# A new stored order and engine choice for the 2207 pieces of an attention and gated-MLP kernel

## The chip, the core and the metric

The kernel runs on one core of one Trainium2 chip. The metric is device time in microseconds (us) of one execution, as the median of several runs. The core has a matrix engine (TensorE, PE in the profile, its weight loads shown apart as PEld), a vector engine (VectorE, DVE), an engine for functions such as exp and gelu (ScalarE, ACT), a general engine (GpSimd, POOL) and a queue engine that issues transfers (SyncE, SP). Each engine runs its own instructions in the order in which the program gives them; engines wait for each other with semaphores.

## What is computed

There are 8 batches of 8 heads, 576 positions and 64 columns. Attention is taken twice, once over a band of 7 neighbours and once over means of 4 positions, and the two results are added. The output is the input of a gated MLP (512 to 1024 columns, a 576 x 576 product across positions, 512 to 512) with a residual:

```python
q_d = q.reshape(B, H, Sd, factor, D).mean(axis=3)
out_d = sm_attn(q_d, k_d, v_d)
out_up = np.repeat(out_d, factor, axis=2)
mask = np.abs(pos[:, None] - pos[None, :]) < factor
out_local = np.matmul(attn, v)
return (out_up + out_local).astype(np.float32)
```

```python
h = x @ w_in            # then gelu
u, v = (h[..., :d_ff // 2], h[..., d_ff // 2:])
v_n = (v - mu) / np.sqrt(var + 1e-06) * g_ln
v_s = np.einsum('ts,bsd->btd', w_sg, v_n) + b_sg[None, :, None]
gated = u * v_s
return (x + gated @ w_out).astype(np.float32)
```

## The kernel before

**Pieces and order.** The whole work is cut into 2207 named pieces. `add(name, engines, emit, after, takes, gives)` records one: the engines that may do it, the function that writes its instructions, the pieces it must follow and the buffers it takes and frees. A string, `ORDER`, holds all the names in one sequence; `name/V`, `name/A`, `name/P` or `name/S` chooses DVE, ACT, POOL or SP, and a name alone takes the first engine of its dictionary. `place` reads the string and hands out buffers from three pools (`SIZES`: 8 of PSUM, 10 and 40 of SBUF); a buffer is handed to the next piece that wants one in the order of the string. Then the pieces are written out in that sequence, so the string is the order of work on every engine's queue:

```python
for t, e in order:
    t.emit(e)
```

**Attention** runs over 32 pairs of heads, g = 0 to 31, four per batch. `lq`, `lk`, `lv`, `lw` load; `qs`, `ks` (L394 on DVE, else POOL) and `vs` sum groups of four; `YS` (for the first four pairs `Y` and `S`) are the pooled and the banded scores on PE (L447, L427); `ma`, `mb` add the mask (L435), `mx`, `my` take maxima (L458, L468), `nx`, `ny` scale them (L465, L477 on DVE), `ea`, `eb`, `ec` are the exponentials on ACT (L486, L493), `re`, `rc` the reciprocals, `np`, `nq` the normalizations (L507, L510). `T`, `U`, `t` transpose on PE (L513, L523), `pa`, `pb`, `pc`, `pe` copy the results out of PSUM (L226), `d` and `D` are the two products with the values on PE (L559, L580), `od` (L568), `xa`, `xb` (L587) join them. `xh`, `xl` (L599), `xc` split the result into a high and a low part, since each product of the MLP is made of three reduced-precision matmuls.

**The MLP** of batch b has 5 pieces `v` (L681, five tiles of positions; for batch 0 three of them are cut into `vk` and `v`), each followed by gelu (`vg`), statistics (`vb`, L711), a root (`vp`, L722 on POOL), `vn` (L730) and a split `vh`, `vl` (L750); then 8 pieces each of `u`, `s` and `o` (L759, 128 x 288 outputs, 12 to 14 matmuls). `ua` is the gelu of `u` (L777), `sa` the bias of `s` (L796), `sm` the gate (L803), `gh`, `gl` (L815) the split of the gated value, `oa` the residual (L831), `os` the store. Every `o` needs all four `gl` of its batch.

**Weights** come as 64-bit floats and are turned into a high and a low part by `weight64` for each of 24 blocks: `wb` (L301, L303) on DVE, `wu`, `wq` on ACT, `wf` (L318) on DVE, `wt` (L323) on POOL, `wh` (L226) and `wl` (L329) on either of two engines. Letters y, z and r stand for the two halves of the first weight and for the last one. The 576 x 576 weight has five `whq`, `wlq` (L356). All of it is done during batch 0.

So in the first 100 us or so the weights, the attention of batches 0 and 1 and the MLP of batch 0 are interleaved, and later the attention of one batch with the MLP of the one before.

Of the kernel before, what the change touches and what calls it, by code (L numbers as in the profile page):

```python
# [92 lines left out]
wqy6 wuy6 nq0/P T0 re1/V t0 U0 nx2/V pa0/V rc1 ea2 wur3 wuz2 wur0 wbz4 pb0/V qs3/V wqz4 wfy6 pc0/V ks3/V pe0/V S3
mx3 wbz5 wfz4 eb2 wuz3 nx3/A wur7 ea3 wly4/P wly3/P nq1/P np1/P T1 pa1/V U1 wqz5 wly5/P wty6/P d0 qs4/P lv2 re2/V
why6/V t1 pb1/V rc2 wby1 pc1/V od0 wqy1 lq5 Y3 wfz5 pe1/V ks4/P wfy1 D0 np2/P eb3 xa0 xb0 T2 my3 pa2/A wuz5 wur1
wur2 ny3/A wuz1 nq2/P U2 wtz4/P wty1/P YS4 pb2/V xh0/V pc2/V t2 wuz0 why1/A ma4 mb4 wbz7 pe2/A ec3 wqz7 d1 mx4 nx4/A
b lw4 re3/A wq3 eb4 lq6 wly6/P my4 wbz6 d2 xl0/P wly1/P wtz5/P xc0 rc3 lv3 wr4 lk6 od1 lv4 lw3 qs5/P lk5 D1 wbz0
nq3/P wfz7 ny4/V wqz6 np3/P wfz6 wtz7/P od2 xa1 wqz0 wq0 wfz0 D2 xb1 xa2 xh1/V ec4 ea4 re4/A xb2 xl1/V wtz0/P wtz6/P
t3 rc4 np4/V vk2.0 T3 vk1.0 pa3/A wbz2 wur4 wbz1 ks6/V U3 pb3/A pc3/A whz7/A pe3/A vk1.1 vk2.1 xh2/A T4 pa4/A nq4/P
wqz1 U4 wqz2 pb4/A whz6/A wlz7/P d3 pc4/A od3 xc1 t4 xl2/P pe4/A qs6/V ks5/V wfz2 wfz1 vs4 wlz6/V whq3/A whz5/A  # L100
vk1.2 wlz5/P whq2/A whz4/A D3 xa3 xb3 xh3/A whz0/A YS5 xc2 wtz1/P vk0.0 lq7 lk7 wur5 xl3/P lv5 wq4 wq1 wlz4/P xc3
ma5 mb5 mx5 wtz2/P qs7/P my5 wbz3 ny5/V d4 vk0.1 vk2.2 vk0.2 v0.1 v0.2 od4 nx5/A eb5 wbr1 wqz3 wfz3 v0.0 wtz3/P
wlq2/P ec5 whz1/A wqr1 ks7/V D4 ea5 wbr5 v0.4 whz3/A wqr5 whz2/A xa4 wfr1 wbr3 xb4 wr6 lw6 v0.3 re5/A va0.4/A wqr3
wfr5 rc5 wbr2 vj0.4 wfr3 wtr1/P wlz1/P wlz3/P vg0.0 np5/P u0.4 T5 vg0.2 vg0.1 vg0.4 vg0.3 wqr2 whq4/A wlz0/V vb0.0
vb0.2 wlz2/V nq5/P u0.6 ua0.6 ua0.4 whr1/A pa5/A wur6 whq1/A whq0/A vb0.1 YS6 vp0.0 wlq3/P u0.0 U5 xh4/A ua0.0
wlq4/V u0.1 vn0.0 wlr1/V vp0.1 vh0.0/A vn0.1 ma6 vb0.3 wtr5/P t5 wtr3/P wlq0/P whr3/A vh0.1/A ua0.1 whr5/A pb5/A
pc5/A vp0.2 vb0.4 wlq1/V wlr3/V vn0.2 mb6 vp0.4 u0.3 u0.7 u0.2 lq8 lw5 pe5/A vp0.3 vn0.4 vh0.2/A vl0.0/V vh0.4/A
# [10 lines left out]
v1.2 vg1.1 vb1.1 vp1.1 vn1.1 ks10/V pe8/A re9/A rc9 np9/P nq9/P vg1.2 d8 od8 v1.0 vg1.0 vg1.3 vb1.2 vp1.2 D8 u1.0
lv9 os0.1 vb1.0 T9 xa8 vp1.0 vn1.0 vs9 vb1.4 xb8 vb1.3 vp1.4 ks11/V vn1.2 vn1.4 u1.2 ua1.2 U9 u1.3 YS10 ua1.0 pa9/A
vp1.3 vh1.0/A pb9/A lk12 lw10 vh1.4/V ma10 my10 mb10 vn1.3 vh1.3/V pc9/A xh8/V ua1.3 ny10/V vl1.4/V lq12 mx10 nx10/V  # L120
vl1.3/V u1.4 qs12/V t9 ua1.4 u1.1 pe9/A d9 vh1.1/A vh1.2/A od9 ua1.1 u1.5 vl1.1/P qs11/P D9 u1.7 ec10 xl8/P xc8 xa9
xb9 xh9/V vl1.0/V vl1.2/P ks12/V eb10 ea10 YS11 lw11 lv10 u1.6 s1.4 lk13 lq13 my11 ma11 ny11/A ec11 re10/V rc10
np10/V T10 mb11 mx11 xl9/V nq10/P s1.0 U10 pa10/V qs13/V pb10/V pc10/V sa1.0 ua1.5 nx11/A ua1.6 ua1.7 s1.1 sa1.1
ks13/V t10 xc9 vs10 s1.2 sm1.1/P pe10/V d10 sm1.0/V ea11 eb11 re11/A s1.3 sa1.2 sm1.2/P rc11 gh1.0/A s1.5 sa1.4
np11/V lv11 gl1.0/P nq11/V U11 T11 sa1.3 s1.6 od10 t11 pa11/A sm1.4/P pb11/A pc11/A sm1.3/V sa1.5 sm1.5/V gh1.2/A
gh1.1/V gl1.1/V pe11/V sa1.6 vs11 gl1.2/V s1.7 sa1.7 sm1.6/P D10 d11 xa10 xb10 sm1.7/P od11 YS12 gh1.3/A D11 lq14
lv12 ma12 xa11 xb11 mb12 gl1.3/P my12 xh10/V ny12/V vs12 YS13 ma13 mb13 my13 lk14 o1.7 o1.6 o1.2 xh11/A o1.4 lw13
# [847 lines left out]
```

## Time and profile before

| | us |
|---|---|
| median of 3 runs | 598.51 |
| lowest and highest | 598.5 and 599.11 |
| span of the profiled execution | 597.5 |
| PE, DVE, ACT, POOL busy | 574.8, 433.8, 333.1, 319.4 |

The page's rows in tenths cut the span into 40 slices of 14.9 us each. A row of a waits view names who waited, on which line, for whom; a row of a stretches view gives the length of the stretch, then for PE, PEld, DVE, ACT and POOL the busy time and the number of instructions, then the granted clock of PE, the share of the DMA engines and GB/s. A row of the chain of waits has a start, a length and the engine, tile and line, with a count where several instructions stand together. A group row has the engine, operation, output and input, shapes and count, then busy time and the mean ns of one, then the idle time before them.

### The profile page before, as it was taken

The page shows a single profiled execution, that of the slowest core. Times are in us where ns is not written, and L with a number is a line of the kernel's source. Part 1 is how long each engine was busy: PE and PEld are TensorE (multiplying, and loading weights), DVE is VectorE, ACT ScalarE, POOL GpSimd, SP SyncE. Part 2 cuts the span into 40 slices and gives each one's busy share as a digit, 9 for nine tenths or more (in the row PEclk, how much of TensorE's full clock was granted, in tenths as well). Part 3 has the DMA queues.
Part 4 walks back from the last instruction along what each step waited for, and adds up shares of the span by engine and source line. Part 5 has one row for each costly group of instructions (what it writes and reads, how often), then busy time and mean ns, then how long its engine had stood idle before and what let it go on. Part 6 is the DMA issues. An engine that isn't in the chain of part 4 may idle for free.

```text
span 597.5 us, 16612 instructions
## 1 busy us (share of the span) xinstructions
PE 574.8 (96%) x6544; PEld 524.0 (88%) x6544; DVE 433.8 (73%) x926; ACT 333.1 (56%) x1264; POOL 319.4 (53%) x407
## 2 busy tenths in 40 slices
PE   3889998999999999999999999999999999999997
PEld 2577997988999899988999889998999989998997
DVE  5999999867786787745966587964879659753553
ACT  5999974764937357371475547548484635722210
POOL 4888889534764154742765364625766336431330
PEclk9989998999999999999999999999999999999999
DMA  8996105072031150502213432403404030010002
GB/s 307 359 276 195 58 15 172 22 225 84 22 101 67 40 186 1 174 20 82 73 48 122 142 105 64 123 34 104 149 25 147 2 122 23 22 42 20 21 21 80
DMA packets 28494, 58.18 MB, mean 97 GB/s; under 512 B 3328, under 2 KB 3584, under 8 KB 28416
## 3 DMA queue, kind: packets, MB, share of 16 engines
q1 hardware_dynamic: 27840, 55.88, 29.5%
q8 instruction: 52, 0.85, 0.6%
q10 hardware_dynamic: 576, 1.23, 0.6%
q14 instruction: 26, 0.21, 0.1%
HBM read 47.66 MB, written 9.44 MB: 96 GB/s over the span
## 4 chain that ended last, share of the span: by engine, by line
PE 86%; DVE 6%; ACT 4%; issue 2%; POOL 1%; DMA 1%; DVEq 0%; POOLq 0%; ACTq 0%
PE ps L759 49%; PE ps L681 18%; PE ps L580 4%; PE ps L559 3%; PE ps L523 3%; PE ps L513 3%; PE ps L427 3%; PE ps L447 3%; ACT X L486 3%; DMA R<-in_qT_dram 1%; DVE R L803 1%; ACT R L309 1%; DVE vs L796 1%; POOL R L803 1%; DVE R L750 0%
## 5 line engine op out<-in xcount | busy, mean ns | idle before, releaser
L759 PE MATMUL ps<-wsg_h,R 128*128 128x288 f32 x576 | 122.3, 299 | 0.0
L759 PE MATMUL ps<-R,wout_h 128*128 128x288 f32 x512 | 110.1, 301 | 0.0
L486 ACT ACTIVATE X<-X,nb 128x64 f32<-128x64 f32 x280 | 93.5, 339 | 6.0 <-DVE nb L465 5.7
L759 PEld LDWEIGHTS ps<-wsg_h,R 128*128 128x128 f32 x576 | 93.7, 188 | 0.7 <-ACT R L226 0.2
L759 PE MATMUL ps<-wsg_l,R 128*128 128x288 f32 x320 | 92.6, 295 | 0.0
L759 PEld LDWEIGHTS ps<-R,wout_h 128*128 128x128 f32 x512 | 84.1, 189 | 2.2 <-issue 1.0
L759 PE MATMUL ps<-X,win_h 128*128 128x288 f32 x256 | 78.7, 308 | 0.0
L759 PE MATMUL ps<-R,win_h 128*128 128x288 f32 x256 | 75.7, 296 | 0.0
L759 PE MATMUL ps<-R,wout_l 128*128 128x288 f32 x256 | 75.7, 296 | 0.0
L759 PE MATMUL ps<-X,win_l 128*128 128x288 f32 x256 | 75.6, 295 | 0.0
L722 POOL TENSOR_TENSOR rs<-rs,nhalf 128x1 f32<-128x1 f32 (+1 forms) x40 | 24.9, 628 | 79.2 <-DVE rs L713 79.2
L681 PE MATMUL ps<-win_h,X 128*128 128x512 f32 x160 | 65.6, 410 | 0.0
L681 PE MATMUL ps<-win_l,X 128*128 128x512 f32 x160 | 63.1, 395 | 0.0
L759 PEld LDWEIGHTS ps<-wsg_l,R 128*128 128x128 f32 x320 | 60.3, 188 | 0.0
L803 POOL TENSOR_TENSOR R<-R,vs 128x288 f32<-128x288 f32 x31 | 29.6, 963 | 45.1 <-DVE vs L796 40.4
L486 ACT ACTIVATION_READ_ACCUMULATOR X<-X,nb 128x1 f32 x280 | 53.6, 192 | 0.0
L226 ACT COPY R<-ps 72x288 f32<-72x288 f32 (+3 forms) x82 | 32.2, 419 | 37.4 <-PE ps L513 17.4
L796 DVE SCALAR_TENSOR_TENSOR vs<-ps,small_sb,b_sb 128x288 f32<-128x288 f32 x64 | 32.1, 510 | 28.4 <-PE ps L759 24.9
L681 PE MATMUL ps<-win_h,R 128*128 128x512 f32 x128 | 50.6, 395 | 0.0
L759 PEld LDWEIGHTS ps<-X,win_h 128*128 128x128 f32 x256 | 48.2, 188 | 2.1 <-issue 0.6
L759 PEld LDWEIGHTS ps<-R,win_h 128*128 128x128 f32 x256 | 48.3, 189 | 0.3
L759 PEld LDWEIGHTS ps<-R,wout_l 128*128 128x128 f32 x256 | 48.4, 189 | 0.0
(100 smaller groups left out, 1405.9 us busy)
## 6 DMA issues: line engine op xcount, KB each, us to landing
X<-in_vw_dram SPq DMA_DIRECT2D x31, 320.0 KB
R<-in_v_dram SPq DMA_DIRECT2D x64, 144.0 KB
R<-in_kT_dram SPq DMA_DIRECT2D x31, 293.0 KB
out_dram<-R SPq DMA_DIRECT2D x31, 288.0 KB
R<-in_qT_dram SPq DMA_DIRECT2D x30, 293.0 KB
R<-in_w_in_dram SPq DMA_DIRECT2D x16, 256.0 KB
...
```

What stands on the lines that cost most here:

```text
L226: (nc.scalar.copy if e == "A" else ENG[e].tensor_copy)(**kw)
L427: nc.tensor.matmul(out=sp[i][os, c * KB:(c + 1) * KB], lhsT=q[hs, t * QB:t * QB + KB], rhs=k[hs, t * QB:t * QB + KB], start=not early, sto ...
L447: nc.tensor.matmul(out=st["sdv"][n][os], lhsT=qd2[par][hs, i * 48:i * 48 + HD], rhs=st["kd"][hs], start=True, stop=True)
L486: nc.scalar.activation(out=st["ms"][:, t, :], in_=src, func=AF.Exp, bias=st["nb"][:, t:t + 1], scale=scale, accum_out=sums[par][:, t:t + 1])
L513: nc.tensor.matmul(out=out, lhsT=st["ms"][0:LD, 2 * c:2 * c + 2, :], rhs=turn_l, is_transpose=True, start=True, stop=True)
L523: nc.tensor.matmul(out=out[:, i * QD:(i + 1) * QD], lhsT=st["pd"][0:QD, n, keys], rhs=turn_p[:, i % 2], is_transpose=True, start=True, sto ...
L580: nc.tensor.matmul(out=at["ps", "o", g, i][hs, c * QB:(c + 1) * QB], lhsT=v[ks, c, hs], rhs=pt[ks, c, h ^ int(2 * c + i >= NA)], start=Tru ...
L681: nc.tensor.matmul(out=acc, lhsT=r32(l), rhs=r32(w[:, k, DM:DF]), start=(i == 0 and ks[0] == 0), stop=(i == len(ops) - 1 and ks[-1] == KT ...
L722: nc.gpsimd.tensor_tensor(out=rs[0:n], in0=rs[0:n], in1=nhalf[0:n], op=ALU.pow)
L759: nc.tensor.matmul(out=acc[:, 0:HALF], lhsT=r32(l), rhs=r32(r), start=(first and n == 0), stop=(last and n == len(ops) - 1))
L796: nc.vector.scalar_tensor_tensor(out=vsb[i], in0=at["ps", "m", b, "s", i][:, 0:HALF], scalar=g_sb[:, i // 2:i // 2 + 1], in1=b_sb[:, half( ...
L803: ENG[e].tensor_tensor(out=u[:, half(i)], in0=u[:, half(i)], in1=vsb[i], op=ALU.mult)
```

## The change

The string `ORDER` is replaced by another sequence of the same 2207 names, with other engine suffixes on some of them. All functions that write instructions, all dependencies and the pool sizes are as before. In `weight64`, `wt` loses DVE from its dictionary; every `wt` of the old string had `/P`, so the engine is POOL in both. By piece, the counts of engines that change (before to after): `gh` on ACT 18 to 14; `gl` on POOL 13 to 18; `ks` on POOL 11 to 15 and `qs` 15 to 18; `np` on POOL 16 to 19, `nq` 21 to 18; `nx` on ACT 16 to 18, `ny` 17 to 14; `pa` on ACT 25 to 17, `pb` 18 to 21, `pc` 17 to 20; `re` on ACT 24 to 21; `sm` on POOL 31 to 28; `wh` on DVE 3 to 9 (of the 24 fp64 blocks); `wl` on DVE 7 to 11; `xl` on POOL 17 to 19.

The diff, cut to its start, the place of the first MLP's gate (`sa0.7`, `gl0.3`, `o0.6`), and `weight64`:

```diff
--- before.py
+++ after.py
@@ -85,116 +85,114 @@
 
 
 ORDER = """
-wy2 wby2 wy0 wy7 lq0/A lk0/A wby0 wuy0 wuy2 wqy2 wby7 wfy2 wy4 small wqy0 wy3 wy5 lq1/A lk1/S wy1 lk2 lq2 wfy0 wz7
-lq3 wy6 wz5 lv0/S lk3 wz4 wz2 wz6 ks0/V wr3 qs0/P wqy7 wr0 wr2 Y0 wuy7 S0 lq4 lk4 wz3 wr7 wz1 lw0/S wr1 lv1/S wz0
-lw1/A wfy7 wby4 wty0/P wuy4 why0/A wty2/P why2/A wqy4 wty7/P my0 why7/A ny0/A wuy3 wfy4 wby3 wby5 wly0/P mx0 wty4/P
-wuy5 ec0 wqy3 why4/A wfy3 wqy5 ks1/V wfy5 qs1/P wly7/P wuy1 ks2/P qs2/V nx0/A ea0 eb0 S1 wuz7 mx1 wr5 lw2 wq2 wty5/P
...
-vs5 xl4/P wbr6 ec6 wqr7 whr2/A nx6/A wlr5/V wqr6 s0.1 wfr7 sa0.1 wfr6 s0.2 s0.0 s0.4 wqr4 wfr4 s0.3 wtr7/P wtr4/P
-sm0.1/P eb6 ea6 re6/A wbr0 sa0.0 sm0.0/P wlr2/V wqr0 rc6 sa0.2 wfr0 sa0.3 wtr6/P sm0.2/P gh0.0/A gl0.0/V whr4/A
-sm0.3/V s0.5 sa0.4 sa0.5 sm0.4/V whr6/A whr7/A gh0.1/A s0.6 sm0.5/V sa0.6 nq6/V s0.7 gh0.2/A d5 sm0.6/V sa0.7
-sm0.7/V lv6 lk8 np6/P wtr0/P wlr4/P wlr7/P T6 t6 od5 whr0/A gh0.3/A pa6/A D5 YS7 gl0.1/V xa5 gl0.3/V ma7 xb5 gl0.2/P
-lw7 my7 wlr6/P lk9 xh5/A wlr0/P mb7 mx7 U6 nx7/V pb6/V ny7/A ec7 o0.6 o0.7 pc6/V pe6/V o0.3 oa0.6 ks8/V ea7 eb7 lq9
...
-os6.3 sa7.6 sm7.6/P gh7.3/V gl7.3/V o7.6 o7.2 o7.3 o7.1 o7.0 oa7.2 oa7.3 o7.4 oa7.0 oa7.1 oa7.4 o7.5 oa7.6 oa7.5
-os7.0 o7.7 oa7.7 os7.1 os7.3.0 os7.2 os7.3.1
+wy2 wuy2 wby2 wy4 wuy4 wby4 wqy2 wfy2 wty2 wy0 wuy0 lk0/A wqy4 lq0/A qs0/P wy7 small wy3 wby0 lk1/S ks0/V wqy0 wfy0
...
+wqr3 wfr3 wtr5 wur3 wtr3 vb0.0 vp0.0 whq4/A vk1.2 v0.1 vg0.1 vb0.1 wtr7 vk2.2 v0.2 v0.4 va0.4/A vj0.4 vn0.0 qs6/P
+vg0.2 vb0.2 whr3/A v0.3 wlr3/V vp0.2 vg0.3 vb0.3 T5 U5 whq1/A wlq1/V pa5/A vn0.2 wur0 vp0.1 vn0.1 pb5/A pc5/A whr7/A
+wlq4/V vp0.3 vn0.3 u0.0 ua0.0 u0.1 ua0.1 whr5/A u0.4 ua0.4 YS6 ma6 lk8 vg0.4 vb0.4 vh0.0/A vl0.0/P vh0.3/A vl0.3/V t5
+pe5/A mb6 wbr6 wlq3/V vh0.1/A vp0.4 vn0.4 whr2/A xh4/A wlr5/P wqr6 wfr6 u0.6 ua0.6 u0.5 vl0.1/V vh0.2/A vl0.2/V u0.3
+u0.7 ua0.7 vh0.4/A u0.2 vl0.4/V ua0.2 ua0.3 wbr0 wqr0 wlr2/P wbr4 wqr4 mx6 wfr0 ua0.5 wfr4 wtr6 whr6/A vs5 lq8 wlr6/P
+my6 ny6/V wlr7/V ec6 nx6/A qs8/V ea6 wtr0 s0.0 sa0.0 s0.1 sa0.1 sm0.1/V s0.2 whr0/V wlr0/V sm0.0/V gh0.0/V gl0.0/V
+sa0.2 wtr4 whr4/A sm0.2/V s0.3 sa0.3 sm0.3/V d5 wlr4/V od5 eb6 re6/V rc6 np6/V gh0.1/A gl0.1/V s0.4 lv6 vs6 sa0.4
+sm0.4/V s0.6 sa0.6 s0.5 sa0.5 sm0.5/V nq6/P sm0.6/P s0.7 sa0.7 t6 D5 YS7 gh0.2/A sm0.7/V gh0.3/V xa5 xb5 xh5/A lw7 my7
+lq9 T6 U6 pa6/A pb6/V pc6/A pe6/A gl0.2/P gl0.3/V o0.6 xl5/P lk9 ma7 mb7 mx7 xl4/V xc5 ny7/A ec7 d6 lv7 od6 o0.7 oa0.6
+oa0.7 ks8/P os0.3 nx7/A ea7 eb7 re7/A ks9/V D6 lw8 qs9/V xa6 xb6 xc4 rc7 YS8 lk10 my8 lq10 ma8 mb8 mx8 vs7 o0.3 o0.0
+np7/P T7 ny8/A ec8 nq7/P ks10/V qs10/P pa7/V U7 nx8/A ea8 pb7/A t7 pc7/V pe7/A xh6/V xl6/P oa0.0 eb8 re8/A rc8 np8/P
...
@@ -333,7 +331,7 @@
         add(f"wu{t}", {"A": 0.36}, units, [f"w{t}"])
         add(f"wq{t}", {"A": 0.34}, square, [f"wb{t}"])
         add(f"wf{t}", {"V": 0.43}, flush, [f"wq{t}"], takes=keys[1:2], gives=keys[2:])
-        add(f"wt{t}", {"P": 0.75, "V": 0.7}, total, [f"wf{t}", f"wu{t}"])
+        add(f"wt{t}", {"P": 0.75}, total, [f"wf{t}", f"wu{t}"])
         add(f"wh{t}", {"A": 0.36, "V": 0.26}, high, [f"wt{t}"])
         add(f"wl{t}", {"P": 0.9, "V": 0.36}, low, [f"wh{t}"], gives=keys[:2])
```

More of the change, by code (lines that the diff above doesn't have):

```diff
@@ L93 @@
[L93 to L107, printed above, removed]
@@ L118 @@
[L118 to L127, printed above, removed]
@@ new lines @@
+xc12 u2.0 ea15 s2.1 sa2.1 T14 nq14/P re15/A vs14 lq17 rc15 oa1.1 pa14/A U14 pb14/A pc14/V ua2.0 t14 pe14/V ks17/P
+np15/V os1.0 nq15/V ua2.2 sa2.0 sm2.0/V u2.1 ua2.1 sm2.1/P s2.2 sa2.2 d14 lv15 od14 U15 T15 pa15/V pb15/A D14 xa14
+YS16 my16 ny16/V ec16 ma16 mb16 xb14 pc15/A mx16 lq18 nx16/V vs15 eb16 xh14/V xl14/V ea16 lk18 ks18/P qs18/V t15
+pe15/V s2.3 s2.4 qs17/V re16/V gh2.0/A rc16 u2.3 ua2.3 u2.4 ua2.4 d15 lv16 od15 np16/V nq16/V T16 sa2.3 lw16 sm2.2/P
+sa2.4 pa16/V lw15 sm2.4/V U16 vs16 pb16/A pc16/A t16 pe16/A xc13 D15 YS17 lq19 xa15 xb15 ma17 mb17 mx17 nx17/V qs19/V
@@ new lines @@
+eb18 re18/A rc18 vg3.2 lw19 my19 ny19/V ec19 mx19 nx19/A np18/P nq18/V vs18 vb3.2 ea19 xh17/V vp3.2 vn3.2 vl3.0/P v3.3
+o2.7 vg3.3 vb3.3 vp3.3 o2.3 vn3.4 o2.2 oa2.2 ks21/P vn3.3 oa2.3 eb19 vh3.4/A vl3.4/V os2.1 vh3.2/V vl3.2/V vh3.3/A
+vl3.3/V xl17/V qs20/P xc17 U18 T18 pa18/A pb18/V re19/A pc18/A qs21/V rc19 nq19/V o2.4 oa2.4 o2.5 oa2.5 os2.2 o2.6
+oa2.6 o2.0 np19/V oa2.0 s3.1 s3.0 u3.0 t18 T19 pa19/V oa2.7 pe18/A d18 lv19 os2.3 od18 U19 pb19/V sa3.1 t19 ua3.0
+sa3.0 pc19/A sm3.0/V pe19/A vs19 u3.3 u3.1 s3.3 s3.2 u3.2 ua3.2 s3.5 sa3.2 u3.5 ua3.3 o2.1 u3.4 oa2.1 s3.4 ua3.1
@@ L198 @@
+o7.7 o7.0 o7.4 oa7.4 os6.2 o7.5 oa7.5 os7.2 ok3 o7.2 oa7.2 o6.6 o7.3 oa7.3 os7.1 o7.6 oa7.6 oa6.6 oa7.7 os7.3.1 o6.7
+oa6.7 os6.3 ok1 o7.1 os7.3.0 oa7.0 oa7.1 os7.0
 """
```

158 lines of the change are left out of this document (84 added, 74 removed).

## The prediction

> **What bounds the kernel now.** I read the first part of the page for the whole, the page's slices for places, then the waits of the TensorE (PE), the stretches and the chain of waits.
>
> ```profile
> PE 574.8 (96%) x6544; PEld 524.0 (88%) x6544; DVE 433.8 (73%) x926; ACT 333.1 (56%) x1264; POOL 319.4 (53%) x407
> ...
> PE   3889998999999999999999999999999999999997
> ...
> DVE  5999999867786787745966587964879659753553
> ```
>
> PE is busy 96% of a span of 597.5 us, so most of the time can only fall if PE's own pieces get cheaper. But DVE shows a 9 in slices two to seven (15 to 105 us), and nowhere else in a row: there the two engines are level. The waits say how far PE suffers from it:
>
> ```profile
> PE ps L447 <- POOL R L323: 10.0, 1, 10.0
> PE ps L523 <- DVE R L510: 1.9, 1, 1.9
> PE ps L513 <- ACT X L486: 1.6, 1, 1.6
> ...
> PE ps L447 <- DVE vs L796: 0.5, 1, 0.5
> ```
>
> The first is the start (nothing to multiply until 10.0 us). The second and the last belong to the stretch from 95 to 101 us shown below. The others are small and scattered. So of before there are three regimes: start-up to 45 us, a stretch to about 103 us in which DVE and PE are both full, and 490 us in which PE alone counts. The stretches:
>
> ```profile
> 44.00:65.00 21.00, 21.00 (x248) 16.40 (x247) 19.87 (x45) 19.53 (x72) 18.82 (x25) 1.00 0.56 159
> 65.00:95.00 30.00, 30.00 (x271) 29.63 (x271) 28.79 (x58) 22.55 (x70) 25.60 (x29) 1.00 0.18 54
> 95.00:100.40 5.40, 3.22 (x64) 2.20 (x62) 5.40 (x9) 1.95 (x4) 4.30 (x5) 1.00 0.77 220
> 100.40:103.80 3.40, 3.14 (x54) 2.99 (x55) 3.37 (x7) 1.12 (x2) 3.32 (x5) 0.50 0.64 175
> ...
> 131.00:200.00 69.00, 68.75 (x796) 62.52 (x795) 51.01 (x111) 41.51 (x155) 36.07 (x45) 1.00 0.21 64
> ```
>
> The columns after the length are busy time of PE, its weight loads, DVE, ACT and POOL, then the granted clock. From 44 to 100.4 us DVE is busy 19.87 + 28.79 + 5.40 = 54.06 of 56.4 us, in 45 + 58 + 9 = 112 instructions: 0.483 us each, and only 2.3 us free. From 95.0 PE is idle 2.2 of 5.4 us, and the 3.4 us behind that run at half the clock. From 131 us on DVE is busy 51.01 of 69 us: no bound any more. The chain of waits carries the same through single instructions:
>
> ```profile
> 71.32 0.33 DVE wout_l L329
> ...
> 75.56 0.34 DVE wout_l L329
> ...
> 85.95 1.62 DVE wout_l L329
> ...
> 96.01 0.81 DVE R L803 x2
> ...
> 98.60 1.58 DVE R L803
> 100.18 0.44 DVE vs L796
> 100.62 0.04 issue
> 100.66 0.76 PE ps L447 x8
> ...
> 103.64 2.42 PE ps L759 x17
> ```
>
> Two things are to be seen. At 100.66 us PE's scores of head pair 7 (`YS7`) start when DVE has finished `sa0.7`, the last bias of the first batch's gate; the first output product, `o0.6`, follows at 103.64. And one instruction, L329 on the same shape, takes 0.33 us or 1.62 us, L803 0.41 or 1.58: the long ones fall where POOL is busy.
>
> **The change part by part.** The 6544 matmuls, loads and stores are the same; only the stored order and the engine of some pieces differ. I counted both orders.
>
> *PE's switches.* A dense product (u, s, o, v) is cheaper behind another dense product than behind attention in fp32, and the small attention pieces differ too:
>
> ```profile
> 138.36 0.74 PE ps L580 x40
> 139.10 1.79 PE ps L759 x12
> ...
> 141.31 1.60 PE ps L759 x12
> ...
> 217.04 0.58 PE ps L580 x40
> ...
> 315.51 0.29 PE ps L523 x3
> ...
> 316.54 0.41 PE ps L523 x3
> ```
>
> The u product takes 1.79 us behind an A·V (L580) and 1.60 otherwise: 0.19 apart. L580 takes 0.74 behind a dense piece and 0.58 behind scores: 0.16. A transposition (L523) is 0.29 among dense pieces and 0.41 among attention: 0.12 the other way. The new order gathers attention: dense pieces straight behind fp32 attention fall from 48 to 23 (25 x 0.19 = 4.75 us saved), fp32 pieces straight behind `D` or `YS` rise from 15 to 35 (20 x 0.16 = 3.2 saved), and transpositions followed by attention rise from 29 to 69 (40 x 0.12 = 4.8 lost). Sum 3.2 us saved, nearly all behind 103 us, where PE is the bound, so it counts in full. Bounds: 6 us if the transpositions lose only a quarter of it (the other pairs are unseen in before's trace), 0 if they lose half as much again and a fifth less is saved.
>
> *DVE before the first gate.* Up to `sa0.7` before stores 158 words for DVE, the new order 175. PE's work stored ahead of that place is about the same. By name 37 come in and 20 go out. Net of those that cancel: six fp32 casts of weights (`wh`, L226), four `wl` (L329), one `wlq` (L356), three `pe` and two `pa` copies, two gates `sm` (L803), the half-tile `vl0.4` (L750), one `gl` (L815), one `gh` (L226) come in; one `pc` copy, one `nq` (L510) and two `ny` (L477) go out. Prices, mean over the run:
>
> ```profile
> L815 DVE TENSOR_TENSOR R<-R,R 128x576 fp32r<-128x576 f32 x19 | 17.1, 899 | 1.0 <-ACT R L226 0.7
> ...
> L226 DVE COPY R<-ps 72x288 f32<-72x288 f32 x29 | 12.8, 442 | 0.0
> ...
> L510 DVE TENSOR_TENSOR R<-R,rc 128x432 f32<-128x432 f32 x11 | 9.5, 865 | 0.1
> L226 DVE CAST R<-R 128x576 fp32r<-128x576 f32 x14 | 9.2, 661 | 3.5 <-POOL R L803 3.1
> ...
> L477 DVE TENSOR_SCALAR nbd<-stats 128x3 f32<-128x3 f32 x15 | 7.6, 505 | 0.1
> ...
> L226 DVE COPY R<-ps 128x464 f32<-128x464 f32 x7 | 4.4, 632 | 3.6 <-PE ps L513 3.6
> L750 DVE TENSOR_TENSOR R<-R,R 64x512 fp32r<-64x512 f32 x5 | 4.3, 867 | 0.1
> L226 DVE COPY R<-ps 128x116 f32<-128x116 f32 x14 | 3.8, 270 | 3.7 <-PE ps L523 3.4 <-issue 0.3
> ...
> L356 DVE TENSOR_TENSOR wsg_l<-R,wsg_h 128x576 fp32r<-128x576 f32 x2 | 1.5, 758 | 0.0
> ...
> L226 DVE CAST win_h<-R 128x256 fp32r<-128x256 f32 x3 | 0.8, 279 | 0.0
> ```
>
> With the short prices of L329 (0.34) and L803 (0.41): 6 x 0.279 + 4 x 0.34 + 0.758 + 3 x 0.270 + 2 x 0.632 + 2 x 0.41 + 0.867 + 0.899 + 0.661 - 0.442 - 0.865 - 2 x 0.505 = 6.8 us. With the stretch's mean instead, 17 x 0.483 = 8.2. Both are time on an engine that had 2.3 us free in 56.4. I take the lower price, since the new order moves some of this work off POOL, so that fewer of the long cases should arise, and let half of the free time take a part: 6.8 - 1.2 = 5.6 us later at `sa0.7`. Bounds: 1 us (all free time is used, and the long cases shrink by a third) and 9.6 us (20 words at 0.483: the new order has three more DVE words between `sa0.7` and `gl0.3`, which the first o product, `o0.6`, needs). In before that product starts 3 us behind `sa0.7`, so PE cannot pass this place in the new order before DVE does. What the wait holds up: PE's queue is in order, so `YS7`, `T6`, `U6` and everything after them slide with it. The 1.9 us of `t6` and the 0.5 of `YS7` are inside before's 100.66 and so are not saved beside it.
>
> [...]
>
> *The start.* The loads of the first `k` and `q` are issued by ACT behind its first weight pieces, so PE's 10.0 us wait gets longer, by an estimated 0 to 1.7 us. I cost it at nothing: DVE and ACT have weights to convert meanwhile, and DVE is the later one at 100 us. Without that cover it is 1.7 us.
>
> *Behind 103 us.* Before's waits of PE behind that are the scattered ones (1.6 and smaller). I followed the buffers and results of the new order and found about as many places where a result is short of time by a little; I take them as equal, with 2 us either way, the size of the longest above. ACT alternates between exp and gelu 40 times instead of 28:
>
> ```profile
> L493 ACT ACT_TABLE_LOAD x8 | 10.3, 1283 | 6.6 <-DVE nbd L477 6.5
> L777 ACT ACT_TABLE_LOAD x7 | 9.0, 1283 | 0.1
> ```
>
> 12 x 1.283 = 15.4 us more of ACT, beside an ACT that was busy 41.51 of 69 us (131 to 200): hidden, at nothing; if ACT were the bound it would be up to 15.4. [...]
>
> **Sum.** 597.5 + 5.6 - 3.2 + 0 + 0 = 599.9 for the profiled span. The median of the runs, 598.51, stands 1.0 above that span, so 600.9: slower by 0.4%.
>
> **The rivals.**
> 1. *DVE is no later than before* (the other side, faster). The price of contention falls as POOL's pieces move to DVE, and DVE's order lets PE's needs pass first. For it: POOL was busy 25.60 of 30 us beside the long DVE instructions. Against it: the chain ran through DVE from 70 to 100 us, with 17 words fewer. It decides below 3.2 us of extra DVE time at `sa0.7`: at 0 the span is 597.5 - 3.2 = 594.3, and where DVE is early enough that the idle 2.2 us at 95 us and half of the 3.4 us at half clock go too, 594.3 - 2.2 - 1.7 = 590.4, so 591.4 to 595.3 in the median.
> 2. *It cancels.* DVE loses 2 to 4.4 us: 597.3 to 599.7.
> 3. *Contention at its full price, or new waits.* 9.6 us instead of 5.6 at `gl0.3`, and 2 us of new waits: 600.9 + 4.0 + 2 = 606.9.
>
> **How the numbers follow.** Within 0.2% (about what a measurement of this kernel can tell from no change) is 597.3 to 599.7. My forecast (599.7 to 604) has 0.36, rival 3 (604 to 608) 0.14: slower 0.50. Rival 2 has 0.17. Rival 1 has 0.33: this is a sum of differences of engines that are level, and a switch saving at its bound of 6 us or a third fewer long DVE cases would turn the sign. The range leaves out a tenth at each end: 588.6 (rival 1 with 2.8 us more of switches, its bound) to 606.9. The likeliest case's own range is 599.7 to 604.
>
> **What would show it.** Right: PE in the new profile waits on DVE for several us around `T6`, `YS7` and `o0.6`; `o0.6` starts at 107 us or later, from 103.6; DVE shows 9 through 105 us; the stretch behind it is about 3 us shorter for the same work. Wrong: PE passes `o0.6` before 103 us; or the long L329 and L803 become rare; or PE's waits behind 103 us grow by more than 2 us, above all on ACT behind a table load.

## The result: 3.1% slower, and where the profile puts it

| | before | changed order |
|---|---|---|
| median of the runs, us | 598.81 | 617.40 |
| lowest and highest | 598.50 and 600.39 | 615.44 and 620.06 |
| span of the profiled execution | 597.5 | 613.7 |

The ratio is 1.0312, with a 95% interval from 1.0281 to 1.0342. The forecast was 600.9 and its range ended at 606.9. The sign was right; the size, and most of the reasons, were not, so the right sign was luck.

First the page of the changed kernel: busy time, and the slices (40 of 15.3 us) of PE, DVE, ACT and of PE's granted clock.

```profile
PE 574.8 (94%) x6544; PEld 522.9 (85%) x6544; DVE 426.2 (69%) x935; ACT 342.8 (56%) x1261; POOL 321.9 (52%) x420
...
PE   0779999899899999998999999999999999999997
...
DVE  3699999959655787959826876477865787446342
ACT  2599976587634647858524949246762768213100
...
PEclk9879999999999999999999999999999999999999
```

PE is busy for the same 574.8 us as before (its time at half clock included), so in sum the 16.2 us of span that were lost are waits. The first slice has a 0 where before had a 3. Then PE's waits, the largest first (lines are 2 lower than in before):

```profile
PE ps L445 <- POOL qd L396: 17.9, 2, 16.0
PE ps L578 <- ACT od L566: 3.4, 5, 1.6
PE ps L511 <- DVE R L585: 1.9, 1, 1.9
PE ps L418 <- ACT X L484: 1.5, 1, 1.5
PE ps L757 <- ACT R L491: 1.2, 1, 1.2
PE ps L757 <- DVE X L433: 1.1, 2, 0.9
PE ps L445 <- DVE R L316: 1.0, 1, 1.0
```

PE starts at 16.0 us in place of 10.0, and behind that stands a long tail of waits of one or two us, on ACT, DVE and POOL alike. The stretches of the changed kernel:

```profile
15.10:30.00 14.90, 10.91 (x156) 6.84 (x156) 9.86 (x30) 7.14 (x35) 9.84 (x16) 0.90 1.01 324
30.00:44.00 14.00, 11.40 (x160) 8.08 (x161) 13.65 (x36) 12.84 (x76) 11.59 (x15) 0.74 0.75 245
...
131.00:160.00 29.00, 27.77 (x291) 23.91 (x293) 21.96 (x47) 21.62 (x78) 18.70 (x26) 1.00 0.32 107
160.00:200.00 40.00, 39.10 (x496) 36.51 (x487) 23.18 (x50) 19.04 (x71) 24.30 (x32) 1.00 0.25 74
200.00:300.00 100.00, 96.19 (x1137) 87.11 (x1135) 79.34 (x168) 70.07 (x254) 61.43 (x81) 1.00 0.29 93
300.00:400.00 100.00, 98.84 (x1028) 92.78 (x1029) 59.90 (x130) 51.03 (x172) 44.81 (x58) 1.00 0.26 81
400.00:500.00 100.00, 98.07 (x1235) 88.59 (x1234) 74.50 (x163) 58.20 (x218) 53.03 (x71) 1.00 0.28 89
```

And of before, for the same times behind 200 us:

```profile
200.00:300.00 100.00, 98.31 (x1167) 90.56 (x1167) 71.44 (x150) 48.50 (x176) 50.44 (x63) 1.00 0.29 90
300.00:400.00 100.00, 100.00 (x1154) 93.06 (x1153) 72.98 (x148) 58.58 (x245) 48.34 (x61) 1.00 0.28 87
400.00:500.00 100.00, 100.00 (x1155) 90.13 (x1154) 71.99 (x152) 55.17 (x196) 57.10 (x74) 1.00 0.27 87
```

From 131 to 500 us PE idles 1.23 + 0.90 + 3.81 + 1.16 + 1.93 = 9.0 us in the changed kernel and 0.25 + 1.69 = 1.9 in before. ACT's busy time from 200 to 300 us rises from 48.5 to 70.1.

Single pieces can be followed by name through all traces, since the names fix the order on every queue. Two orders can be compared only at a piece ahead of which PE has done the same set of pieces in both. Starts of such pieces, in us, with two of the experiments beside them:

| piece | PE pieces ahead of it | before | changed | e2_head_before | e5_loads_first_lw1_sp |
|---|---|---|---|---|---|
| `Y0`, first scores | 0 | 10.0 | 16.0 | 10.2 | 10.0 |
| `vk2.1` | 30 | 47.1 | 58.3 | 46.5 | 50.5 |
| `v0.4` | 47 | 60.5 | 71.8 | 60.0 | 64.0 |
| `o0.6`, first output product | 75 | 103.3 | 114.1 | 102.4 | 106.9 |
| `d11` | 133 | 176.4 | 188.7 | 178.3 | 181.9 |
| `YS24` | 292 | 386.3 | 402.3 | 391.0 | 394.9 |
| from `o0.6` to the end | | 494.1 | 499.6 | 500.4 | 499.9 |

Of 16.2 us, 11.3 are lost before `vk2.1`, in the first 50 us. From there to `o0.6` nothing is lost (0.5 is won back). The other 5.4 are lost behind `o0.6`, where I had forecast a gain of 3.2, and nearly all of it between `o0.6` and `YS24`. From `vk2.1` to `o0.6` lies most of the stretch in which DVE was to be the bound. It takes 56.3 us in before, 55.8 in the changed kernel and 56.4 in e5_loads_first_lw1_sp; the rows are in this order:

```profile
47.05:103.32 56.27, 53.83 (x614) 48.32 (x612) 53.93 (x107) 42.31 (x134) 49.72 (x58) 0.97 0.35 103
```

```profile
58.33:114.09 55.76, 53.01 (x613) 47.75 (x612) 53.51 (x117) 38.97 (x125) 40.67 (x49) 1.00 0.23 67
```

```profile
50.50:106.88 56.38, 53.39 (x613) 47.72 (x612) 54.55 (x117) 38.81 (x125) 40.65 (x49) 1.00 0.25 73
```

DVE has ten more instructions here and is busy about as long as in before, since some of them became shorter. The gate `sm` and the split `wl` on DVE, in the same stretch, before and then changed:

```profile
L803 DVE TENSOR_TENSOR R<-R,vs 128x288 f32<-128x288 f32 x5 | 5.4, 1086 | 0.0
...
L329 DVE TENSOR_TENSOR wout_l<-R,wout_h 128x256 fp32r<-128x256 f32 x4 | 3.3, 814 | 0.0
```

```profile
L801 DVE TENSOR_TENSOR R<-R,vs 128x288 f32<-128x288 f32 x7 | 3.6, 515 | 0.2
...
L327 DVE TENSOR_TENSOR wout_l<-R,wout_h 128x256 fp32r<-128x256 f32 x4 | 1.9, 470 | 0.0
```

POOL is busy 40.7 us of the stretch in place of 49.7.

### The profile page after: what moved, and what is told of

Same layout as the page of the kernel before. It is cut to its first block, busy times and chain, and to the rows that moved or that the text cites. A ratio compares the mean times of both kernels' runs of the same rounds, so it can differ in the third digit from the quotient of the medians.

```text
span 613.7 us, 16663 instructions
## 1 busy us (share of the span) xinstructions
PE 574.8 (94%) x6544; PEld 522.9 (85%) x6544; DVE 426.2 (69%) x935; ACT 342.8 (56%) x1261; POOL 321.9 (52%) x420
## 3 DMA queue, kind: packets, MB, share of 16 engines
q10 hardware_dynamic: 576, 1.23, 0.5%
## 5 line engine op out<-in xcount | busy, mean ns | idle before, releaser
L757 PE MATMUL ps<-X,win_h 128*128 128x288 f32 x256 | 76.4, 298 | 0.0
L775 ACT ACTIVATE R<-ps 128x288 f32<-128x288 f32 x64 | 24.3, 411 | 60.6 <-PE ps L757 56.5
L801 POOL TENSOR_TENSOR R<-R,vs 128x288 f32<-128x288 f32 x28 | 23.1, 825 | 62.0 <-DVE vs L794 33.6
L224 ACT CAST R<-R 128x512 fp32r<-128x512 f32 (+2 forms) x36 | 22.9, 639 | 49.6 <-DVE R L728 16.9
L679 PE MATMUL ps<-win_h,R 128*128 128x512 f32 x128 | 50.5, 395 | 0.0
```

The lines of the kernel that those rows point to most:

```text
L224: (nc.scalar.copy if e == "A" else ENG[e].tensor_copy)(**kw)
L679: nc.tensor.matmul(out=acc, lhsT=r32(l), rhs=r32(w[:, k, DM:DF]), start=(i == 0 and ks[0] == 0), stop=(i == len(ops) - 1 and ks[-1] == KT ...
L757: nc.tensor.matmul(out=acc[:, 0:HALF], lhsT=r32(l), rhs=r32(r), start=(first and n == 0), stop=(last and n == len(ops) - 1))
L775: nc.scalar.activation(out=us[i // 2][:, half(i)], in_=at["ps", "m", b, "u", i][:, 0:HALF], func=AF.Gelu_apprx_tanh)
L801: ENG[e].tensor_tensor(out=u[:, half(i)], in0=u[:, half(i)], in1=vsb[i], op=ALU.mult)
```

## The experiments

All times are medians; the kernel before was measured again beside each group of experiments.

| run | us | before beside it | ratio, 95% interval |
|---|---|---|---|
| e1_loads_first | 616.48 | 599.05 | 1.0298 (1.0237 to 1.0359) |
| e2_head_before | 606.91 | 599.05 | 1.0130 (1.0101 to 1.0159) |
| e3_tail_before | 610.89 | 599.05 | 1.0194 (1.0159 to 1.0229) |
| e4_four_hoists | 618.63 | 599.05 | 1.0318 (1.0269 to 1.0367) |
| e5_loads_first_lw1_sp | 612.42 | 599.74 | 1.0199 (1.0167 to 1.0230) |
| e6_lw1_sp | 618.21 | 599.74 | 1.0305 (1.0268 to 1.0342) |
| e7_before_loads_late | 602.74 | 599.74 | 1.0049 (1.0029 to 1.0069) |
| e8_before_gate | 600.76 | 599.74 | 1.0019 (1.0002 to 1.0036) |
| e9_tail_old_engines | 651.45 | 599.54 | 1.0863 (1.0822 to 1.0903) |
| e10_old_order_new_engines | 658.06 | 599.54 | 1.0978 (1.0938 to 1.1019) |
| e11_before_u16_later | 598.12 | 599.54 | 0.9966 (0.9948 to 0.9983) |
| e12_consumers_later | 608.50 | 599.54 | 1.0144 (1.0108 to 1.0179) |
| e13_tables_v3 | 605.94 | 598.93 | 1.0115 (1.0080 to 1.0150) |
| e14_tables_all | 604.94 | 598.93 | 1.0105 (1.0067 to 1.0142) |
| e15_gate_words_back | 611.69 | 598.93 | 1.0207 (1.0176 to 1.0238) |

### Head and tail apart: e2_head_before and e3_tail_before

Both orders hold nearly the same set of pieces in their first 567 words, so that either may be followed by the other's rest.

```diff
 e2: before[0:567] + the changed order without those
 e3: changed[0:567] + the order of before without those
```

> The order of before for its first 567 pieces (through re7, some 115 us: all weights, the MLP of batch 0 to its output products), the changed order for the 1640 that remain; the seam displaces two pieces. Theory (the loss of 18.6 us has two halves: the head costs 10.8, start and the stretch to o0.6; what follows costs 5.4 in spite of cheaper switches, through many short waits): 598.8 + 5.4 = 604.2 (602.5 to 606). Rival 1 (only the head lost, what follows saves the 3.2 us of switches): 595.6. Rival 2 (the part behind lost because it comes in late or displaced by the head): below 600.

> The counterpart: the changed order for its first 567 pieces, the order of before for the 1640 that remain. Theory (head costs 10.8): 598.8 + 10.8 = 609.6 (608 to 611.5). Rival 1 (the head alone lost, and more than it seems): 615 or more. Rival 2 (the head's delay is taken back by slack of the rest): under 605.

Measured: 606.91, 0.9 above its range, and 610.89, inside its own. Both rivals that put the whole loss on one side fall. The head costs some 11.8 us and the rest 7.9, and the two add up (19.7, against 18.6 between the two kernels). In the trace the part behind `o0.6` takes 500.4 us in e2, 499.6 in the changed kernel and 494.1 in before: it is slow whatever stands ahead of it.

### The start: e1_loads_first, e5_loads_first_lw1_sp, e6_lw1_sp, e7_before_loads_late

The timeline of ACT, then of DVE and of POOL in the changed kernel, at the start (start, length, engine, line, operation; in brackets the idle time ahead and what ended it):

```profile
6.08 0.38 ACTq L378 DMA_DIRECT2D R<-in_kT_dram  x1
...
6.53 0.42 ACTq L374 DMA_DIRECT2D R<-in_qT_dram  x1
...
15.26 0.43 ACT L311 ACTIVATE R<-R 128x256 f32<-128x256 f32 x1 [5.84 <-DVE ps L301]
```

```profile
6.99 0.43 DVE L301 SCALAR_TENSOR_TENSOR ps<-R,ps 128x256 int32<-128x256 int32 x1
13.34 0.75 DVE L392 TENSOR_REDUCE kd<-R 128x144 f32<-128x576 f32 x1 [5.92 <-DMA R<-in_kT_dram]
```

```profile
14.79 0.67 POOL L395 TENSOR_TENSOR half<-R 128x288 f32<-128x288 f32 x1 [7.35 <-DMA R<-in_qT_dram]
```

The load of the first `k` is issued at 6.08 us and has landed at 13.34. DVE's next word is `ks0`, so DVE stands still for 5.92 us, and ACT behind DVE for 5.84. The load of the first `q`, issued at 6.53, lands later still: POOL waits 7.35 us for it, and `qs0` on POOL is the last that `Y0` needs. The weights that were to cover the delay stand behind `ks0` in the same queue.

```diff
-wy2 wuy2 wby2 wy4 wuy4 wby4 wqy2 wfy2 wty2 wy0 wuy0 lk0/A wqy4 lq0/A
+lq0/A lk0/A wy2 wuy2 wby2 wy4 wuy4 wby4 wqy2 wfy2 wty2 wy0 wuy0 wqy4
```

> The changed order with one edit: lq0/A and lk0/A, the loads of the first q and k, stand first in the stored order, as the first work of ACT's queue; nothing else moves. Theory (late start): in the changed kernel lk0 is issued at 6.08 us and PE's first scores Y0 start at 16.01 instead of 10.00, because DVE sits in ks0 and ACT in a wait behind it, idle 5.9 us each; so Y0 should start at 10 to 11 us and the time fall by 5 to 6 us, from 617.4 to 611.4 (609.5 to 613). Rival (DVE's 17 extra words bound the head anyway, as the prediction had it): Y0 starts early, but DVE is no earlier at sa0.7 (110.6 us), PE's waits before o0.6 grow by what the start gains, and the time falls by under 2 us.

Measured: 616.48; the trace says why nothing came of it. PE starts at 9.97 us and then stops for 6.4 us at `Y2`. ACT's timeline in this run:

```profile
19.32 0.49 ACT L306 ACTIVATE R<-R 128x256 int32<-128x256 uint32 x1
27.77 0.34 ACTq L386 DMA_DIRECT2D X<-in_vw_dram  x1
28.16 0.76 ACT L310 ACTIVATE R<-R 128x256 f32<-128x256 f32 x2 [8.34 <-DMA R<-in_w_sgT_dram]
```

At 19.8 us ACT comes to the issue of `lw1`. It needs no buffer and no result, but the instruction waits for a completion semaphore. In the changed kernel's program it stands as

```
L387 DMA X_297<-in_vw_dram 128x640 [waits DMAHW4_49]
```

The transfers use eight such semaphores (DMAHW0 to 7) in turn, and number 4 was still held by `wq0`, a load that SP issued at 21.3 us in this run and that landed at 27.8, while the DMA engines were busy throughout (nine tenths or more in every slice of 0.85 us between the two). ACT stood still until then, for 8.34 us, with `wqy6` and `wqy5` behind it. DVE's `wfy6` and `wfy5` wait for these (7.03 us), and free the PSUM buffers that `Y2` takes. With the issue on SP, which has nothing to do but issue, ACT goes on at 19.68 us without a gap (e5, below). In the changed kernel itself ACT is idle for only 3.6 us ahead of the same issue: with the late start it comes to it at 25.6 us in place of 19.8. Its trace has the eight semaphores as 101 to 104 and 106 to 109: `wq0`, issued at 21.84 us on 106, has landed at 28.79, and the issue of `lw1`, which waits for 106, begins at 28.81.

So there are two stalls in a row. The next two runs take out both, and the second alone:

```diff
-wz7 lw1/A wz2
+wz7 lw1 wz2
```

> The changed order with two edits: lq0 and lk0 first, as in e1_loads_first, and lw1 (the load of the band's values for pair 1) issued from SP's queue in place of ACT's. In e1_loads_first Y0 started at 9.97 us, yet Y2 stayed at 29.19 (30.21 in the changed kernel) and the time fell by 0.9 us only: ACT sat idle 8.34 us ahead of lw1's issue, which waits for the landing of an earlier load (wq0), and wqy6, wqy5, wfy6, wfy5 and the PSUM buffer for Y2 come behind it. Theory (two stalls in a row, each enough to hold the head): with both gone Y2 starts at 22 to 24 us, o0.6 at 108 to 109 (114.0 in both kernels before it), the time at 610 to 611. Rival (DVE's extra words hold the gate anyway): Y2 early, o0.6 at 112 or later, the time at 614 or more.

> The changed order with lw1 issued from SP alone; lk0 and lq0 stay late. Theory of two stalls in a row: Y0 at 16.0 as in the changed kernel, Y2 at 28 to 29 (30.21), a gain of 1 to 2.5 us: 615 to 616.4. If instead lw1 alone had been the cause and the late start costs nothing, Y2 comes at 24 or earlier and the time at 611 or less.

Measured: 612.42 with both edits, 618.21 with the second alone. Both expectations missed (610 to 611, and 615 to 616.4). Neither edit alone gives anything that can be measured; together they take 5.0 us from the median. In the traces it is 7.0 from the span (613.7 to 606.7) and 7.2 from the start of `o0.6` (114.1 to 106.9), but that is more than the edits are worth: the profiled execution of e5 took 608.5 us, its other three runs 612.3 to 612.9. It had only 3.4 us at half clock in the head, where the changed kernel had 10.2. How much that can do is seen in e15 (below), whose order is the same as that of e5 up to `v0.4`. Between 25.6 and 39.3 us PE did 141 matmuls there and 204 in e5, and `v0.4` started 3.8 us later. The rows of e15 and of e5:

```profile
25.60:39.30 13.70, 12.58 (x141) 10.08 (x141) 10.49 (x26) 10.63 (x61) 9.60 (x12) 0.50 0.96 281
```

```profile
25.60:39.30 13.70, 11.49 (x204) 8.77 (x204) 13.22 (x35) 12.59 (x72) 11.30 (x15) 0.88 1.00 300
```

So the two stalls together are worth some 5 us, with 7 in the one trace. The stretches of e5:

```profile
15.10:30.00 14.90, 10.52 (x163) 6.64 (x162) 14.48 (x39) 11.87 (x69) 12.88 (x19) 0.89 1.05 331
...
65.00:95.00 30.00, 29.78 (x256) 27.82 (x255) 29.21 (x66) 23.24 (x68) 22.82 (x29) 1.00 0.25 71
95.00:106.90 11.90, 9.13 (x146) 8.26 (x144) 11.31 (x22) 2.13 (x7) 3.85 (x3) 1.00 0.01 5
```

DVE is busy 14.48 of 14.9 us behind the start, where the changed kernel had 9.86, and 40.5 of 41.9 us from 65 to 106.9. That looks like the bound that the prediction had. But PE is busy 29.78 of 30 us from 65 to 95 too, and of the 3.6 us by which `o0.6` is later than in before, 3.5 are there at `vk2.1` already (50.5 against 47.1). PE's largest single wait before that is 2.7 us in `S3`, for a PSUM buffer that `ec1` on ACT frees. I did not take these 3.5 us apart.

> The order of before with one edit: the issues of lk0 and lq0 stand behind wuy2 and wqy2 on ACT's queue, about where the changed order has them, in place of the first. Theory (the late start is a price of its own wherever nothing else stalls the head): Y0 at 15 to 16 us in place of 10.0, o0.6 4 to 6 us later than 103.3, the time 603 to 605. Rival (the head of before is bound by ACT and DVE up to 100 us, so the start is hidden): Y0 late, o0.6 within 1.5 us of 103.3, the time under 600.5.

The counterpart in before's order (`lk0/A` behind `wuy2`, `lq0/A` behind `wqy2`): 602.74, a loss of 3.0 us (ratio 1.0049), just under the expected 603. `Y0` starts at 14.4 us, 4.4 later, and `o0.6` at 106.5, 3.2 later. The late loads do cost time where no other stall covers them, but some of the delay is caught up.

### The waits behind 115 us, taken one by one: e4_four_hoists and e12_consumers_later

```diff
 e4:  od9 directly behind d9; ec18 behind od17; d23 od23 ahead of ec24; ma28 ahead of ny28
 e12: v3.3 ahead of D17; u2.1 ahead of T14; u1.1 ahead of D9; u1.2 ahead of T10; o4.1 ahead of D23
```

> The changed order with four local edits on ACT's and DVE's queues, PE's own order untouched: od9 directly behind d9, od17 ahead of ec18, d23 and od23 ahead of ec24, ma28 ahead of ny28. In the changed kernel these four stand 0.4 to 7 us ready behind another piece of their engine, and PE waits for them at D9 0.68, D17 1.69, D23 0.83 and o5.4 1.14 us, 4.3 in sum. Theory (the waits behind 150 us are places where a short piece that PE needs is stored behind long ones, each by itself): 617.4 - 4.3 = 613.1 (612 to 614.5), and those four waits are gone from the trace. Rival (the engines are level there, so the wait only moves to the next piece): less than 1.5 us, with new waits of the same sum beside them.

Measured: 618.63, no gain. The profiled execution of e4 had a slower head (14 us in a row at half clock, shown below), so I read it from `v2.0` on: `v2.0` to `o7.0` takes 387.1 us, in the changed kernel 387.5. All four waits are gone as intended. Three of them lie in this part (`D9` stands ahead of it), and their 3.7 us became 0.4 us of time. Two of its runs had a mean clock of 0.98 and took 621 us; the other two, at 0.99 as in the changed kernel, took 616.0 and 616.3.

> As e2_head_before with five swaps on PE, each setting one dense product ahead of an attention piece that PE waits for: v3.3 ahead of D17 (1.7 us waited), u2.1 ahead of T14 (0.7), u1.1 ahead of D9 (0.7), u1.2 ahead of T10 (0.6), o4.1 ahead of D23 (0.8), 4.5 in sum. Theory (bunching: ACT and DVE are the bound across the whole stretch from the v products to the s products, so the wait moves): under 1.5 us gained, 605.5 to 607. Rival (each wait is local, one product too early): 602.5.

Measured: 608.50, against 606.91 for its base, no gain either. Here PE comes to `D17` one product later and does not wait; it waits at `o2.7` (0.5) and in `s3.1`, the product ahead of `s3.0` (1.7 in place of 0.8), instead. Its profiled execution was the longest of four. From `v3.0` to `s3.0` the changed kernel, e2, e4, e5 and e12 take 28.59, 28.58, 28.59, 28.59 and 28.59 us. That is the sign of a chain that does not run through PE at all: move PE's pieces or single producers, and the stretch keeps its length.

### Engines or sequence: e9_tail_old_engines and e10_old_order_new_engines

```diff
 e9:  e2, with before's engine for 271 pieces behind the first 567
 e10: the order of before, with the changed engine for the same 271 pieces
```

> As e2_head_before (order of before for 567 pieces, changed order behind), but the pieces behind have the engines that before gave them: 271 choices undone, the sequence of every piece kept. ACT still alternates 40 times between exp and gelu. In e2_head_before the part behind o0.6 took 500.5 us, in before 494.1, though its PE pieces are some 3.7 us cheaper; PE's waits there are 14.9 against 4.4. Theory (the sequence does it: attention gathered on PE bunches the work of ACT and DVE, so that they bound short stretches): the time stays at 606.9, within 2 us. Rival (the engine choices do it, more work on POOL and DVE at the wrong places): 602 or less.

> The counterpart: the sequence of before throughout, but the same 271 pieces behind the first 567 have the engines of the changed kernel. PE's order is that of before, ACT alternates 28 times. Theory (the sequence does it): 599.7, within 2 us. Rival (engine choices): 603 or more. If both this and e9 are slow, choices and sequence fit each other and neither is the cause alone.

Measured: 651.45 and 658.06. Both expectations fall. Either order is far worse with the other's engines: by 44.5 us (e9 against e2) and 58.5 us (e10 against before). As I read it, the engine of a piece fits the place where it stands, and a swap at one place delays all that is stored behind it; that was not shown. Part of the loss is PE's clock: in e9 its mean was 0.961 where e2 had 0.993, and PE was busy for 593.4 us in place of 573.2, so some 20 of the 49.4 us of span are slower matmuls. The pair cannot say which half is to blame, as the last sentence of the expectation allows; undoing half of a jointly chosen schedule tells nothing of that half.

### ACT's table loads: e13_tables_v3 and e14_tables_all

ACT's timeline of the changed kernel between `v3.0` and `s3.0`, rows of table loads, of the gelu of `v` (L691) and of `od` (L566) alone:

```profile
275.79 0.60 ACT L691 ACTIVATE R<-ps 128x512 f32<-128x512 f32 x1 [2.20 <-PE ps L679]
...
279.24 1.28 ACT L491 ACT_TABLE_LOAD   x1 [1.85 <-DVE nbd L475]
...
281.62 0.41 ACT L566 ACTIVATE od<-ps 128x288 f32<-128x288 f32 x1
...
285.60 1.28 ACT L691 ACT_TABLE_LOAD   x1
286.89 0.60 ACT L691 ACTIVATE R<-ps 128x512 f32<-128x512 f32 x1
...
288.16 1.28 ACT L491 ACT_TABLE_LOAD   x1 [0.67 <-DVE nbd L475]
...
292.24 1.28 ACT L691 ACT_TABLE_LOAD   x1
293.54 0.60 ACT L691 ACTIVATE R<-ps 128x512 f32<-128x512 f32 x1
294.15 1.28 ACT L484 ACT_TABLE_LOAD   x1
```

The exponentials of pairs 18 and 19 stand between the gelus of `v3.2` and `v3.3`, and each change of function costs 1.28 us: five loads in this stretch (before has one). Nothing is seen here beside the load itself: at 285.60 it begins 0.01 us behind the end of the instruction ahead of it, and the gelu follows at 286.89, 0.01 us behind its end. `v3.3` ends at 286.8 us; its gelu runs at 293.5, and the normalization, `vh3.3`, `vl3.3` and `s3.0` come behind it. `od17`, which `D17` waits for, stands behind `ec18` and its load. So e13 sets `ec18` behind `od17`, and `vg3.3` directly behind `vg3.2`:

```diff
-ec18 d17 v3.2 od17
+d17 v3.2 od17 ec18
-vg3.2 ... ec19 ... ea19 ... vg3.3
+vg3.2 ... vg3.3 ec19 ea19
```

> As e2_head_before with three moves on ACT's queue between the products v3 and s3, PE's order untouched: ec18 behind od17, and ec19 and ea19 behind vg3.3, which then stands directly behind vg3.2. ACT's alternations between exp and gelu fall from 40 to 38. From v3.0 to s3.0 the changed kernel, e2, e4, e5 and e12 all take 28.5 to 28.6 us, though PE's pieces there need 26.0 and e4 and e12 each took one wait of 1.7 us out. In e2 vg3.3 is ready at 276.3 us and runs at 282.9, behind ec19, ea19 and two table loads of 1.28. Theory (ACT's chain with its table loads sets the stretch): v3.0 to s3.0 takes 26.2 to 27.2 us and the waits at D17 and s3.0 go. Rival (DVE's chain sets it, 23.9 of 28.6 us busy): 28 us or more.

```profile
264.10:291.30 27.20, 27.09 (x296) 23.71 (x295) 24.30 (x51) 18.67 (x68) 16.80 (x21) 1.00 0.20 58
```

In e13 the stretch takes 27.2 us in place of 28.6 and PE is busy 27.09 of it; in e2 it was busy here:

```profile
262.20:290.80 28.60, 26.65 (x296) 23.68 (x295) 23.92 (x51) 21.28 (x70) 16.94 (x22) 1.00 0.17 55
```

DVE does the same work (23.9 and 24.3 us), ACT 2.6 us less: two loads. That the wait at `D17` is gone now shortens the stretch, and it did not in e4 and e12. So in this stretch ACT's queue was the chain, and DVE's load was not. The edit takes two table loads away and also sets the gelu ahead of the exponentials `ec19` and `ea19`, so the share of the loads alone is not shown. The median, 605.94 against 606.91, moves by less than the interval can tell.

> e13 with the same done at two more places (ec22 behind ua4.0, ec30 behind vg6.2: 34 alternations in place of 40) and the four hoists of e4 (od9, d23 with od23, ma28). PE's order is that of e2_head_before. Theory (where the table loads no longer stand in the way the hoists pay): PE's waits behind o0.6 fall from 14 us in e2 to 9 or 10, the part behind o0.6 from 500.5 to 496, the time from 606.9 to 602 to 603.5. Rival (the bunching of DVE's work holds it): 605.5 or more.

Measured: 604.94; the rival's bound was 605.5, the theory's 603.5. `v3.0` to `s3.0` again takes 27.2 us. Elsewhere the regrouping only moved the waits: with `ec22` and `ec30` later, PE waits at `u4.2` (1.0) and at `o5.1` (1.2), where it did not in e2, and PE's idle time behind `o0.6` is 9.6 us, in e2 10.0. What sets the other stretches is not settled; I did not try them one by one.

### The gate of the first batch: e15_gate_words_back and e8_before_gate

> e5_loads_first_lw1_sp (the changed order without its two stalls at the start) with six of DVE's extra words of the first gate given back to POOL, as before has them: sm0.0, sm0.1, sm0.2, wlr0, wlr4, wlr7. In e5 o0.6 starts at 106.9 us, in before at 103.3. Theory (what is left of the head's delay is DVE's extra work, 17 words more up to sa0.7): o0.6 at 104 to 105 and the time at 609.5 to 610.5, from 612.4. Rival (POOL is as full, or the gate then waits for POOL): o0.6 at 106.5 or later, no gain.

Measured: 611.69 against 612.42, with `o0.6` at 111.2 us. No gain, as the rival had it, though the trace of e5 is a lucky one to compare with. This execution was already later at `Y3` (38.3 us, e5 35.1), ahead of the first edited word, and from `s0.0` to `o0.6` it took 23.5 us, e5 23.0. The table above says why there was nothing to gain: from `vk2.1` to `o0.6` the new order loses no time to before.

> The order of before with three hoists at the gate of the first batch: on DVE nq6 ahead of sm0.3 (it is ready at 91.1 us and runs at 98.0, t6 waits 2.1 us for it) and sa0.7 ahead of sm0.6 (ready 97.7, runs 100.1, YS7 waits for it), on ACT pa6 ahead of gh0.3 (ready 96.8, runs 101.8, U6 waits for its buffer). PE's order is untouched. Theory (here a short piece stands behind long ones and DVE has room right behind): t6 at about 96.5, the 3.4 us at half clock behind 100.4 go, the time at 594 to 596.5. Rival (DVE is full up to the first output product, so the time only moves from t6 to o0.6, which needs gl0.3): within 1 us of before.

Measured: 600.76 against 599.74 (ratio 1.0019): no gain in the median. `t6` no longer waits for `nq6`, but `D5` behind it waits 2.0 us for `od5` on ACT. From `s0.0` to `o0.6` the profiled execution takes 18.2 us, before 19.1, so 0.9 of the hoped three or more came at the gate; this execution reached `s0.0` 3.6 us later than before's did, in a part of the order that the edit does not touch, so the two rivals are not told apart cleanly.

### A version that beats both: e11_before_u16_later

```diff
-o2.6 U16 o2.3
+o2.6 o2.3 U16
```

> The order of before with one swap on PE: o2.3 ahead of U16. In before U16 (257.5 us) waits 0.97 us for np16 and o2.3 behind it 0.60, while o2.3's own inputs are ready at 254.0. Theory (behind 150 us before has slack everywhere, so that a single wait can be taken out): the two waits go, the time falls by 1 to 1.6 us, to 598.1 to 598.7. Rival (the wait moves to the next piece): no change.

Measured: 598.12 against 599.54, ratio 0.9966 (0.9948 to 0.9983). Both waits are gone from the trace. The same kind of edit that gained nothing in the changed order (e12) pays in before's; I take it that the engines behind PE have room there, which was not shown.

## Why the prediction was wrong, step by step

**The start** (costed at nothing, bound 1.7 us) is the largest miss. The text said that DVE and ACT "have weights to convert meanwhile". They had, but behind `ks0` in the same in-order queue, so the cover was not there: DVE and ACT idled 5.9 us each, POOL 7.4, and `Y0` came 6.0 us later. The bound of 1.7 us, for which the prediction shows no working, was too small as well: the loads of `k` and `q` were issued 4.9 and 5.8 us later than in before (at 6.08 and 6.53 in place of 1.19 and 0.74). The second stall, ACT's issue of `lw1`, was not in the prediction at all. Together they cost 5.0 us of the median and 7.0 of the span in the trace (e5), though neither shows alone (e1, e6).

**DVE ahead of the first gate** (5.6 us) did not come. From `vk2.1` to `o0.6`, with the same work on PE, the new order takes 55.8 us (e5 56.4) and before 56.3. Before's figure holds 2.9 us at half clock; up to 96 us, ahead of that, the changed kernel falls 0.2 us and e5 0.8 us behind. Two steps failed. The price was taken for the 17 new words alone, while the old ones became cheaper: seven `sm` on DVE took 3.6 us where five had taken 5.4. That is the argument of rival 1, and the long L329 and L803 became rare (means of 470 and 515 ns in this stretch, in place of 814 and 1086), which the prediction had named as a sign of being wrong. What makes them long was not shown: in before those at 85.95 and 98.60 us ran beside a POOL instruction of 1.44 and 1.43 us, but POOL was busy beside the short ones at 71.32 and 75.56 too. And the 5.6 us were charged to `o0.6` in full, though the prediction's own rows have PE busy 21.00 of 21 and 30.00 of 30 us from 44 to 95 us. `o0.6` did come behind 107 us, as foretold, but for another reason: PE waits no longer around `YS7` and `U6` (0.6 and 1.9 us) than before at `t6` and `YS7` (1.9 and 0.5). (In before `YS7` and `o0.6` start at 99.7 and 103.3 us; the 100.66 and 103.64 of the prediction are rows of the chain that lie inside them.)

**Behind 103 us** (no change in waits, 2 us either way) is the second miss, and the prediction had named it as a sign of being wrong. PE's idle time from 131 to 500 us went from 1.9 to 9.0. I had counted places where a result is short of time and found as many in both orders. In before a single wait could be taken out (e11); in the new order the next wait takes the place of the one removed (e4, e12, e14). Which chains set the stretches other than that from `v3.0` to `s3.0` stays open.

**ACT's table loads** (hidden, at nothing) were wrong at least between `v3.0` and `s3.0`, where two of them, with the order of ACT's queue around them, cost 1.3 us of 28.6 (e13). The cover that I named, ACT's free time over 69 us, is a mean: in that stretch ACT was busy 21.3 of 28.6 us and in-order behind its loads. That the twelve extra loads cost more elsewhere was not shown.

**PE's switches** (3.2 us saved) came in part: the part behind `o0.6` grew by 5.4 us while PE's idle time there grew by 7.5 (1.9 to 9.4), so the pieces themselves took 2.0 us less. The saving was real and was outweighed. The prediction's bounds for it do not follow from their conditions, which give 6.75 and -0.8 in place of 6 and 0.

By the medians, the 18.6 us are 5.0 for the two stalls at the start (e5), 7.9 for the part behind `o0.6` (e2) and some 6 for the rest, which the traces put into the first 50 us and no experiment took apart. The traces of the changed kernel and e5 have 7.0, 5.7 and 3.6 for the same three.
